# Eight state loads moved behind the first batch's softmax, and a new written order for the whole program

## The chip, the core and the metric

One core of one Trainium2 chip runs the program. Its time is device time in microseconds (us) from launch to end. The profile shows five engines: TensorE for matmuls (PE, with its weight loads PEld), VectorE (DVE), ScalarE (ACT), GpSimd (POOL) and SyncE (SP). In this kernel SP issues nearly all transfers, ACT issues two of them, and POOL issues those of the states and the stores that add to what lies in memory.

## The reference, cut to what matters

The first half is a cross attention between a sequence and a small set of states, for 8 batches and 8 heads. The second half is a gated layer on its result.

```
scores  = x @ state^T / 8           # B=8, H=8, S=512, Ns=32, D=64
a       = softmax(scores)
xread   = a @ state                 # what the sequence reads from the states
a2      = softmax(state @ x^T / 8)
sread   = a2 @ x                    # what the states read from the sequence
x2      = concat(xread, sread) -> (4352, 512) per token
h       = x2 @ w_in                 # 512 -> 2048
out     = (h * erf(softplus(h))) @ w_out   # 2048 -> 512
```

The weights arrive as 64-bit numbers and are turned into 32-bit ones in the kernel.

## The kernel before, in words

All work is cut into named steps. A step is recorded by `step(name, ...)` (L240) and emitted when its name comes up in the string `ORDER` (L20 to L169), a list of some 2,400 names. `in_order` (L1098) then ties each engine to that order, so the string alone decides which instruction stands before which on each engine; the framework adds the waits that the data need. An entry such as `~2*20` emits 20 matmuls of the identity into bank 2 of PSUM: their results are not used.

The steps that matter here, with their lines in the profile:

- `lx0` to `lx3` (L332) load batch 0 of x, 256 KB each, two on ACT's queue and two on SP's; `lst0` (L337) loads the states of batch 0.
- `x0` to `x3` (L435) transpose x on PE, `x0c` to `x3c` copy the results to SBUF, `s0` and `s0c` (L442) do the same for the states, `q0` and `q1` (L450) are the scores, `tm0`, `tm1`, `ta0`, `ta1` and later `tw0`, `tw1` (L455) are further transposes.
- `max`, `less`, `exp`, `sum`, `inv`, `norm` make the softmax of batch 0, in two halves, on DVE with `exp` on ACT. `norm1` is the last of them. `ta0c` and `ta1c` copy the transposed weights into `y` on ACT.
- A piece of w_in (`i0` to `i7`) or of w_out (`o0` to `o7`) is loaded in two halves of 512 KB on SP (`l0`, `l1`, L380) into one of four raw buffers, then converted by two ACT steps (`a0` L392, `a1` L395) and two DVE steps (`v0` L397, `v1` L399). A raw buffer is loaded again only when its `v1` has read it. `i0` is converted in two parts.
- `n00`, `n01`, `n02`, `n10`, `n12` (L935) multiply the states of batch 0 with pieces of w_in; `h0` to `h7` (L946) make the first hidden block from them and from `y`; each `h` has a softplus (`h0s`, L672) and a copy (`h0c`) on ACT. The banks of `h0`, `h1`, `h2` are used again by `h3`, `h4`, `h5`, so `h3` waits for `h0s` and `h0c`.
- `hold` (L463) is a copy of one column on POOL that reads the transposed x. Behind it on POOL stand `lst1` to `lst8` (L356): the states of batches 1 to 7, one load of 56 KB for each head. `u0` and `u1` (L1031) transpose these states on PE and need all eight loads.
- `rd0` to `rd7` (L519) are the reads `a2 @ x`. For batches 1 to 7 the weights of the read go to memory and back (`kz` L590, then four loads `z`), so `rd` waits for the last `z`. The tile `sn` holds the result of `rd0`.
- `a1xq` to `a7xq` (L345) load x a second time in another layout, sixteen transfers of 64 KB for a batch, in the place where batch 0's transposed x lay; `a1s` (L544) are the scores of batch 1.
- The rest is the two blocks of hidden units, A (batches 1 to 7) and B (0 to 7): `A1m` (L634), `A1f` (L683), `A1p` (L733, L804) and so on, on PE, with their sums on DVE and their softplus, erf and copies on ACT.

The code around the moved steps before the change:

```
            if i == 0:
                step("hold", lambda: nc.gpsimd.tensor_copy(out=sn[:, 0, 0:1], in_=xT0[:, 0, 0, 0:1]))
                for h in range(H):
                    step("lst%d" % (h + 1), load_st, h)
```

Of the kernel before, what the change touches and what calls it, by code (L numbers as in the profile page):

```python
# [20 lines left out]
warm lst0 lx0 lx3 lx2 lx1 i0l0 i1l1 i0l1 s0 x0 x3 x0c s0c i1l0 hold x3c x1 lst4 lst6 x2 x1c i2l0  # L21
lst7 q0 x2c lst2 i0a0 lst5 q01c q1 i2l1 i0a1 q00c lst1 i0v0 tm0 q11c big0 lst3 q10c i0v1 tm1 i3l0
lst8 max0 n00 max1 i0+a1 i3l1 less0 i0+a0 o0l0 less1 n00c0 exp0 i0+v0 exp1 sum0 i1a0 sum1 inv0
i1a1 inv1 norm0 norm1 ~2*20 ta0 i2a0 i1v0 ta1 n00c1 i1v1 ta0c i2a1 i0+v1 ~0*3 n02 ta1c i2v0 o0l1
n02c0 big1 ~6*1 n01 o1l0 i3a0 h0 o1l1 i2v1 n01c0 i3a1 n01c1 o2l1 big i3v0 n10 wt0 o2l0 u0 i3v1
a1xq1 n10c0 wt1 u1 n10c1 h0c wz n12 wn1 n12c1 n12c0 a1xq5 o0a0 wn0 ~4*3 tw1 n02c1 u1c o0a1 tw0
o0v0 h2 y01 tw0c o0v1 tw1c o1a0 rd0 a1xq6 t01 o1a1 o1v0 a1xq0 h1 y02 rn0 a1xq7 o1v1 o2a0 rt0 a1xq4
u0c T1 a1xq3 h0s a1xq2 h1s o2v0 ~6*8 h3 h1c a1tx0 h2c a1x2 h2s o3l0 h4 o2a1 i4l1 a1tx2 i4l0 rc0
y04 h3c i5l0 a1tx3 h5 h3s t02 h4s a1tx1 h4c t04 o2v1 a1s h5s h6 t11 a2xq3 h0e h7 a1c1 h0g a1c0
a2xq5 h4e a1my1 o00 a2xq0 a1tu1 h5c h2e a1my0 yl0 a1tu0 a2xq7 o20 h7c h2g a2xq1 a1mx1 o10 h7s i5l1  # L30
a1mx0 h6s o3l1 a1sb1 a2xq4 A1m a1sb0 h4g a1ex1 a2xq6 a1ex0 h6c a1sm1 o22 i4a1 a1sm0 a1ms a1iz i4a0
a1nm0 a1x3 o12 a1ta0 A1m00 a1ey1 i4v0 a1x0 A1f01 a1nm1 A1m10 A1m11 o02 y11 a1ta1 A1m01 a1x1 A1f0c
A1M1 a2xq2 o3a0 a1ty1 A1f02 y12 a1ey0 A1M2 A1f05 i4v1 A1f0c11 A1f06 o3a1 A1f11 a1ty0 i4k A1f0u2
y14 o14 a1kz i5a1 A1M3 y13 a1iy y03 yk1 A1M4 A1f07 i6l0 o3v0 h6e o04 o3v1 A1f0u3 i5a0 A1f0c22
A1f04 h6g a1z1 A1f03 a1z3 a1z2 o24 a1z0 A1f0c12 A1f0s11 i6l1 i5v0 A1f0c21 A1f0s22 i5v1 A1f15 A1f1c
A1f0s12 A1f16 T2 A1f0s21 i5k i7l1 rd1 t3k T4 t1k o06 A1e0 rn11 rn10 a2tx0 rt1 A1f12 A1f1u2 a2x2
a2tx2 o0c A1f17 rc1 i6a0 o0d A1g0 a2s t2k yk0 A1f1u3 t0k i6a1 o30 a3xq5 i6v0 a2c1 i7l0 A1f1c22
a2c0 A1f14 i6v1 A1f13 a2tu0 A1f1s22 i6k o32 a3xq0 A1f1c11 A1f1c12 A1f1c21 yl1 A1f1s11 a2mx0 o16
a3xq2 A1f1s21 A1f1s12 T3 o5l1 o34 a2my0 A1e1 a2x3 o5l0 a2sb0 o26 a3xq4 a2ms A1g1 o36 a2ex0 i7a0
a2sm0 A2m a2x0 o3c i7v0 i7a1 a2iz A1p10 a2nm0 a2x1 A2m10 a2ey1 i7v1 A2m00 A1p11 A2m11 a2ta0 o4l0  # L40
o1c o4l1 o5a1 i7k A2M1 A2f01 a3xq7 y21 A2m01 A2M2 A2f05 A2f0c y22 o2c A2M3 A2f06 a2ey0 a2ty1 A2f02
y23 A2f0u2 a2ty0 A2f07 A2f0c11 y24 a2kz A1A1 A1pc A2f11 a3xq3 A2f0u3 o4a1 A2f0c22 a3xq1 A2f04 A2M4
A1p50 o4a0 A1A2 a3xq6 A2f0c21 o4v0 o1d A2f03 A2f1c a2z0 a2iy o4v1 a2z3 A2f16 a2z2 a2z1 A1p60
A2f0s11 a3tx0 o4k A2f1u2 yl2 A2f0s22 o6l1 A2f0c12 o2d A2f0s12 A2f17 A1A3 o6l0 A2f0s21 A2f12 A2f1u3
A1A4 rd2 o5a0 A2f15 rn21 a3x0 rn20 a3tx2 rt2 A2f1c11 A2f14 rc2 A2f1c22 a3s o5v0 A2f1s11 o5v1 A2f13
a3x3 a3c1 o3d A1p61 a3c0 A2f1c12 t4k A2f1c21 o7l1 a3my0 A2f1s22 a3x1 A2f1s21 A1p20 t6k a3tu0
A2f1s12 a3mx0 A1p21 a4xq4 A2e1 a3sb0 o5k A3m a4xq1 A1pu2 a3ms A2g1 A2e0 o7l0 a4xq0 A1p70 a4xq7
A2g0 A1p71 a3ex0 a4xq5 o6a0 A1p51 a3sm0 a4xq6 A1pu3 o6v0 A3m00 A1p40 a3iz o6a1 A1pc22 a3nm0 a3ey0
A1p41 A3m10 o6v1 a3ey1 A3m11 a3ta0 A1p30 o6k A3m01 a3x2 A1pc11 A3M1 a3iy A3f01 y31 a3ty0 A1p31
A3M2 A3f0c o7a1 y32 y33 A3M3 A3f06 o7a0 a3ty1 A3f02 A3M4 A3f0u2 a3kz y34 A3f05 A3f0c11 a4tx2 A3f07  # L50
o7v0 A3f11 A3f0u3 A2A3 A2p10 A3f0c22 A3f0s11 a3z0 A2A1 a3z2 A3f04 yl3 A1pc12 t5k A2p11 A3f0c21
a4xq3 t61 o7v1 A3f1c A1pc21 a3z1 A3f16 yk3 A3f0s12 A2A2 a3z3 A3f0s22 A3f12 A1d1 A3f1u2 A1d2 t62
A3f03 t03 a4xq2 A3f1c11 t51 t41 A3f17 A3f1s11 A1d3 A3f0c12 A2pc A2p50 t31 A3f0s21 t21 t42 A3f1u3
A2A4 A3f15 t52 A3e0 rd3 t44 A3f1c22 t22 A3f14 t32 a4x2 rn31 rn30 t34 A3f13 a4tx0 rt3 A3f1s22 A2p51
t24 A3f1c21 A3f1c12 rc3 A3f1s12 t54 t12 A2p60 A3f1s21 t64 A3g0 A2p61 A3e1 t33 t14 a4s t43 A2pu2
A3g1 A2p70 a4c1 a5xq6 a4c0 A1d0 yk2 a4tu0 A2p71 a4x3 a5xq5 A3A1 A4m A2pu3 a4mx0 t53 a4x1 A2p20
a4sb0 a5xq7 A2pc22 a4ex0 A2p40 a4my0 a5xq1 A4m10 A4m11 a4sm0 A4m00 A2p41 A4M1 a4iz A4M3 A2p21
A2pc21 a4nm0 A4m01 t23 A2p30 A2pc11 a4ta0 A2d0 a5xq4 A4M2 A4f01 y41 a5xq0 a4ms A4M4 A2p31 a4ey0
y43 a5xq3 A4f0c y42 a4ty0 a4ey1 A4f06 y44 a4ty1 A4f02 A4f0u2 A3A2 a4kz A3ap10 a4x0 A4f0c11 A2d2
a4iy A3A4 A4f07 a5xq2 A4f05 A3A3 A4f0u3 A4f11 A4f0c22 A2d3 A4f04 a5tx2 A4f0s11 a4z1 A4f03 a4z3  # L60
A4f0c21 a4z2 A2pc12 a4z0 A3ap11 A4f1c A4f0c12 A2d1 A4f16 t13 A4f0s21 A3b1 A3ac A4f12 A4f1u2 t63
a5tx0 A4f15 A4f1c11 A4f0s12 A4f17 A3a1 rd4 A4f1u3 A3b3 A4f0s22 A4f14 a5x3 rn41 rn40 A4f1c22 rt4
A3ap50 A3a2 A4e0 A4f13 A3a3 A3ap60 rc4 A3a4 A3ap61 a5s A4f1s22 A4f1c12 A3au2 A4g0 A4f1c21 A3ap20
a6xq7 A4f1s21 A3ap70 a5c1 a6xq2 a5c0 A3ap71 A3b2 A4f1s12 a6xq5 A4f1s11 A3ap21 a5tu0 A3au3 a5x2
A3ap51 o7k A3ac11 a5my0 a6xq3 A3ap40 A3ac22 A3ap41 A4e1 a5mx0 A3bp10 a5x1 A3b4 A3bp11 a6xq1 A3ac21
a5sb0 A3ap30 A3bc A3ap31 a5ms A4g1 a5x0 A3bp60 a6xq6 a5ex0 A3bp61 A5m A3bu2 a5sm0 yl4 a6xq0 A3b4+
a5iz A3bp20 A3ac12 A5m10 a5nm0 A5m11 A3d0 A3bp21 a5ey0 a6xq4 A3bp50 A5M1 A5m01 A3bp51 a5ta0 A5m00
A3bp70 a5ey1 A3bp71 A5M2 A5f01 y51 A3bu3 A3D0 a5iy A5M3 A3bp40 A5f0c A3bc22 A3bp41 a5ty1 A5f02 y52
a5ty0 A5f06 A5f0c11 y53 a5kz A4A3 A3bp30 A3d3 A5f0u2 A3bc21 A3bp31 A5M4 A3bc11 A5f07 y54 A3bc12
A5f05 A5f0u3 A4A1 A4ap10 A3U2 A5f11 a5z3 A5f0s11 A5f0c22 a5z2 A3d2 A5f04 a6tx2 a5z1 A5f03 a5z0  # L70
A5f0c21 A4A2 A4ap11 A5f1c A3U3 A5f16 A4ac a6tx0 A5f12 A3D2 A5f1u2 A5f0c12 A4ap20 A4A4 A5f0s21
A5f17 A5f0s12 A4a1 A5f15 A5f1u3 A5f0s22 rd5 A3U4 A5f1c22 A5f14 rn50 rn51 A5e0 A4a3 A4ap21 A4a2 rt5
A5f13 rc5 A4ac11 a6s A5g0 A4ap60 a6c1 a7xq1 a6c0 A4ap61 A5f1c12 A5f1c21 yk4 A3d1 A4bp10 a6tu0
A4au2 a7xq6 A5f1c11 A4bp11 A4a4 A4ap70 yk5 a7xq0 A4ap71 a6mx0 A5f1s22 A5f1s12 A4ap50 a6my0 A5f1s11
A4ap51 A4au3 A3D1 a6sb0 a6x1 A4ap40 a7xq2 A3D3 A4ap41 A4ac22 a6ex0 A4b1 A4ap30 a6x0 A4ac21 a6sm0
A4ap31 A4bc A6m A4b2 a6x2 yl5 a6ms a6iz a6ey0 A4b4 A4b3 A4bp60 A6m00 A6m10 a6nm0 A4bp61 a6ey1
A4bp20 A4ac12 A4bu2 A4bp21 a6ta0 A4bp70 A4d2 A4bc11 A4d0 A4bp71 a7xq3 A4b4+ A4bp50 a6iy a6ty1
A5f1s21 a6ty0 A6f01 A6m11 y61 A4bu3 a6kz A4bp51 A6M1 A6m01 a6x3 A4bp40 y62 A6f0c a7xq7 A6M2 A4D0
A4bp41 A6M3 A6f02 A4bc22 A5e1 A6f06 y63 A6M4 A4bp30 y64 a7tx0 a6z3 A6f0c11 A4bp31 a6z2 A6f0u2
A6f05 a6z1 A5g1 a6z0 A6f07 a7xq4 A5ap10 A6f0u3 a7xq5 A6f11 A6f0c22 yk6 A5A3 A4d3 A6f04 A6f0s11  # L80
# [96 lines left out]
def kernel(  # L177
# [8 lines left out]
    nc = tc.nc  # L186
    B, H, S, D = x.shape
# [27 lines left out]
    big = sb("big", 12800)  # L215
# [928 lines left out]
```

## Time and profile before

| | |
|---|---|
| three timed runs, median (lowest to highest) | 697.61 us (697.14 to 698.43) |
| the profiled execution's own time | 698.53 us |
| its span, first to last instruction | 696.8 us |
| what lies around the span | 1.7 us |
| PE busy | 686.2 us (98%) |
| DVE busy, ACT busy | 583.0 us (84%), 487.3 us (70%) |
| POOL busy | 67.4 us (10%) |
| granted TensorE clock, mean of the span | 0.995 |

In the page, busy time is given for each engine with its share of the span. A timeline line gives start, duration, engine, line, operation, output<-input and count, and in square brackets how long the engine was idle before it and what ended that idle time. The ends of matmuls are modelled, so the distance between starts says more than the busy time of PE. A 32-bit matmul shows as two records; a transpose shows as one.

### The profile page before, as it was taken

What the parts mean: (1) busy time and instruction counts of PE and PEld (TensorE: products, weight loads), DVE (VectorE), ACT (ScalarE), POOL (GpSimd) and SP (SyncE); (2) the same over time, 40 slices, a digit from 0 to 9 for tenths busy, and PEclk for the clock granted to TensorE, in tenths of its full rate; (3) what the DMA queues carried; (4) which work ended last, traced back from release to release, by engine and by line L of the source; (5) the groups of instructions that cost most, each with busy time, mean ns of one, the idle gap of its engine ahead of it and who ended that gap; (6) DMA issues with size and microseconds to landing.
All of it is one profiled execution on the core that took longest, in us unless ns stands there. A gap on an engine that the chain in (4) does not pass through costs nothing.

```text
span 696.8 us, 13280 instructions
## 1 busy us (share of the span) xinstructions
PE 686.2 (98%) x5357; PEld 585.7 (84%) x5357; DVE 583.0 (84%) x761; ACT 487.3 (70%) x725; POOL 67.4 (10%) x67
## 2 busy tenths in 40 slices
PE   8899999999999999999999999999999999999997
PEld 7445557787898888899998879898999898998996
DVE  5789998999999999999935779797869796959772
ACT  4799999986696877967236785868576867575720
POOL 3000000000000200220200003020201020111002
PEclk9899999999999999999999999999999999999999
DMA  9988999865657595872456245142432323222516
GB/s 271 280 217 230 283 266 279 206 188 116 167 115 178 121 232 123 163 194 52 71 189 205 62 122 61 54 50 65 47 83 22 78 34 82 33 52 29 101 46 120
DMA packets 144028, 92.09 MB, mean 132 GB/s; under 512 B 92512, under 2 KB 135008, under 8 KB 143712
## 3 DMA queue, kind: packets, MB, share of 16 engines
q1 hardware_dynamic: 129536, 77.16, 39.3%
q0 software_dynamic: 13888, 13.57, 15.5%
q8 instruction: 42, 0.69, 0.4%
q10 hardware_dynamic: 544, 0.52, 0.2%
q14 instruction: 18, 0.15, 0.1%
HBM read 51.12 MB, written 40.11 MB: 131 GB/s over the span
## 4 chain that ended last, share of the span: by engine, by line
PE 84%; ACT 6%; DMA 4%; DVE 3%; SPq 2%; issue 1%; DVEq 0%; ACTq 0%
PE b L804 38%; PE b L683 23%; PE b L733 13%; PE b L1007 4%; PE b L634 4%; DMA ring<-in_moe_w_in_dram 2%; DMA big<-in_x_dram 1%; PE b L519 1%; ACT ring L672 1%; PE b L946 1%; PE b L544 1%; SPq L380 1%; ACT big L395 1%; ACT ring L242 1%; ACT L672 1%
## 5 line engine op out<-in xcount | busy, mean ns | idle before, releaser
L242 ACT COPY ring<-b 128x512 f32<-128x512 f32 (+1 forms) x140 | 80.3, 583 | 74.3 <-PE b L683 59.6
L683 PE MATMUL b<-y,m 128*128 128x256 f32 x480 | 121.3, 380 | 0.0
L711 POOL DMA_DIRECT2D out_dram<-res x52 | 61.6, 1415 | 610.0 <-DVE y L242 203.5
L804 PEld LDWEIGHTS b<-big,ring 128*128 128x128 f32 x928 | 111.5, 192 | 5.7 <-ACT big L582 0.8
L804 PE MATMUL b<-big,ring 128*128 128x128 f32 x928 | 115.1, 275 | 0.0
L242 ACT COPY res<-b 128x512 f32<-128x512 f32 (+2 forms) x118 | 61.2, 528 | 74.7 <-PE b L804 49.1
L683 PEld LDWEIGHTS b<-y,m 128*128 128x128 f32 x480 | 86.9, 190 | 13.4 <-issue 1.3
L683 PE MATMUL b<-sy,m 128*128 128x256 f32 x360 | 91.8, 382 | 0.0
L236 DVE TENSOR_TENSOR ring<-ring 128x2048 f32<-128x2048 f32 (+1 forms) x36 | 77.7, 2164 | 15.2 <-ACT ring L691 8.0
L235 DVE TENSOR_TENSOR ring<-ring 128x1024 f32<-128x1024 f32 (+2 forms) x80 | 86.4, 1086 | 0.3
L672 ACT ACTIVATE ring<-ring 128x512 f32<-128x512 f32 x128 | 77.1, 631 | 4.8 <-DVE ring L234 4.3
L683 PEld LDWEIGHTS b<-sy,m 128*128 128x128 f32 x360 | 64.9, 190 | 10.0 <-issue 0.9
L234 DVE TENSOR_TENSOR res<-res,b 128x512 f32<-128x512 f32 (+2 forms) x56 | 33.8, 604 | 41.0 <-PE b L804 17.5
L234 DVE TENSOR_TENSOR ring<-ring,b 128x512 f32<-128x512 f32 (+1 forms) x71 | 46.8, 660 | 24.9 <-PE b L683 8.0
L733 PE MATMUL b<-ta,ring 128*128 128x256 f32 x280 | 64.3, 381 | 0.0
L804 PEld LDWEIGHTS b<-ta,ring 128*128 128x128 f32 x496 | 60.1, 192 | 3.4 <-issue 1.7
L804 PE MATMUL b<-ta,ring 128*128 128x128 f32 x496 | 62.5, 276 | 0.0
L733 PEld LDWEIGHTS b<-ta,ring 128*128 128x128 f32 x280 | 52.5, 190 | 11.2 <-ACT res L242 2.7
L804 PE MATMUL b<-big,ta 128*128 128x128 f32 x476 | 59.5, 276 | 0.0
L804 PEld LDWEIGHTS b<-big,ta 128*128 128x128 f32 x476 | 56.8, 192 | 3.0 <-issue 2.5
L691 ACT ACTIVATE ring<-ring 128x2048 f32<-128x2048 f32 x30 | 57.1, 1911 | 0.3
L242 ACT COPY b<-b 128x512 f32<-128x512 f32 (+2 forms) x61 | 33.3, 548 | 20.5 <-PE b L733 6.8
(147 smaller groups left out, 1006.1 us busy)
## 6 DMA issues: line engine op xcount, KB each, us to landing
out_dram<-res POOLq DMA_DIRECT2D x48, 256.0 KB, 5.0
out_dram<-res SPq DMA_DIRECT2D x32, 256.0 KB, 3.5
big<-in_x_dram SPq DMA_DIRECT2D x30, 256.0 KB, 4.9
big<-in_x_dram SPq DMA_DIRECT2D x112, 64.0 KB, 3.4
big<-in_moe_w_in_dram SPq DMA_DIRECT2D x12, 512.0 KB, 6.8
big<-in_moe_w_out_dram SPq DMA_DIRECT2D x12, 512.0 KB, 5.7
kept_y<-y SPq DMA_DIRECT2D x8, 512.0 KB, 3.8
y<-kept_y SPq DMA_DIRECT2D x8, 512.0 KB, 3.9
```

Of the source, the lines that this page charges most:

```text
L234: add = lambda o, a, b: tt(o, a, b, op=ALU.add)
L235: sub = lambda o, a, b: tt(o, a, b, op=ALU.subtract)
L236: mul = lambda o, a, b: tt(o, a, b, op=ALU.mult)
L242: do[name] = lambda: f(*args)
L634: pe.matmul(out=to[j][k][Ns * p:Ns * p + Ns, :], lhsT=by, rhs=w_in[r, 4 * j:4 * j + 4, i, :], start=True, stop=True)
L672: act.activation(out=o, in_=i, func=ACTF.Softplus)
L683: pe.matmul(out=to[:, i], lhsT=xs[n - 1][:, q:q + P], rhs=ys[n - 1], start=(start and i == 0), stop=(i == 1), skip_group_check=True)
L691: step(u + "e%d" % o, lambda s=s: act.activation(out=s, in_=s, func=ACTF.Erf))
L711: nc.gpsimd.dma_start(out=to, in_=of, accum_op=ALU.add)
L733: pe.matmul(out=to[:, E2 * h:E2 * h + E2], lhsT=a[:, k // 2, k % 2], rhs=rhs[n][:, k], start=(start and h == 0 and k == 0), stop=(k == 3), ...
L804: pe.matmul(out=out_[:, P * j:P * j + P], lhsT=lhs[:, i], rhs=rhs[:, i], start=(start and j == 0 and i == 0), stop=(i == 1), skip_group_ch ...
L1007: pe.matmul(out=to[:, P * i:P * i + P], lhsT=xs[n - 1][:, i, k], rhs=ys[n - 1][:, k], start=(start and i == 0 and k == 0), stop=(k == 1), ...
```

## The change

Two steps of code and the written order.

```
@@ attention0
             step("x%d" % i, turn, i)
             ...
-            if i == 0:
-                step("hold", lambda: nc.gpsimd.tensor_copy(out=sn[:, 0, 0:1], in_=xT0[:, 0, 0, 0:1]))
-                for h in range(H):
-                    step("lst%d" % (h + 1), load_st, h)
...
             step("ta%dc" % g, act.copy, y[0][:, g], tp[g])
+        step("hold", lambda: nc.gpsimd.tensor_copy(out=sn[:, 0, 0:1], in_=A0[:, 1, 0, 0, 0:1]))
+        for h in range(H):
+            step("lst%d" % (h + 1), load_st, h)
```

`hold` now reads the normalized weights of the first batch (`A0`, second half), so it and the eight state loads behind it on POOL wait for `norm1`.

The string `ORDER` is another one from the first name to the last. It holds the same steps, apart from the unused matmuls: 35 before (in five places) and 43 after (in six places). Its beginning before:

```
warm lst0 lx0 lx3 lx2 lx1 i0l0 i1l1 i0l1 s0 x0 x3 x0c s0c i1l0 hold x3c x1 lst4 lst6 x2 x1c i2l0
lst7 q0 x2c lst2 i0a0 lst5 q01c q1 i2l1 i0a1 q00c lst1 i0v0 tm0 q11c big0 lst3 q10c i0v1 tm1 i3l0
lst8 max0 n00 max1 i0+a1 i3l1 less0 i0+a0 o0l0 less1 n00c0 exp0 i0+v0 exp1 sum0 i1a0 sum1 inv0
i1a1 inv1 norm0 norm1 ~2*20 ta0 i2a0 i1v0 ta1 n00c1 i1v1 ta0c i2a1 i0+v1 ~0*3 n02 ta1c i2v0 o0l1
n02c0 big1 ~6*1 n01 o1l0 i3a0 h0 o1l1 i2v1 n01c0 i3a1 n01c1 o2l1 big i3v0 n10 wt0 o2l0 u0 i3v1
a1xq1 n10c0 wt1 u1 n10c1 h0c wz n12 wn1 n12c1 n12c0 a1xq5 o0a0 wn0 ~4*3 tw1 n02c1 u1c o0a1 tw0
o0v0 h2 y01 tw0c o0v1 tw1c o1a0 rd0 a1xq6 t01 o1a1 o1v0 a1xq0 h1 y02 rn0 a1xq7 o1v1 o2a0 rt0 a1xq4
u0c T1 a1xq3 h0s a1xq2 h1s o2v0 ~6*8 h3
```

and after:

```
warm lx0 lx1 lx3 lx2 lst0 i0l0 i0l1 x0 i2l0 x1 x0c x3 x1c s0 i2l1 x3c x2 s0c q0 x2c i1l0 i0a0 q00c
~7*2 q1 q01c i0a1 i0v0 tm0 i1l1 q10c big0 q11c i0+a0 i0v1 tm1 i0+a1 max0 i3l0 n00 max1 less0 i3l1
less1 exp0 o0l0 i0+v0 exp1 sum0 n00c0 i2a0 sum1 inv0 inv1 i2a1 norm0 norm1 ~2*21 ta0 i1a0 i0+v1
hold ta1 big1 lst7 o0l1 i1a1 i1v0 lst3 n00c1 lst8 ta1c i1v1 ta0c lst6 i3a0 lst4 ~0*8 n01 i2v0 o1l1
n02 lst1 big o1l0 n01c0 i2v1 n02c0 lst5 i3a1 ~2*3 h0 lst2 i3v0 o2l0 o0a1 n01c1 o2l1 n02c1 a1xq7
i3v1 n10 wt0 h1 n10c0 n10c1 wt1 y01 h0c a1xq2 wz n12 wn0 n12c0 n12c1 o0a0 wn1 ~2*3 tw0 y02 tw1
o1a0 u0 tw0c tw1c u1 o1a1 a1xq6 rd0 u1c a1xq0 o0v0 h2 o2a0 u0c a1xq3 rn0 o0v1 a1xq1 rt0 o1v0 a1xq5
h0s o2v0 h1s ~6*6 h3
```

In the loads, x's four transfers now come first and the states of batch 0 last of them; the first four pieces of w_in come in the order i0, i2, i1, i3 (before: i0 and i1 mixed, then i2, i3). On ACT the conversion of i2 now stands before that of i1, and `ta1c`, `ta0c` behind both. On PE, `h1` moves ahead of `n12`, and `u0` and `u1` move from behind `n10` to behind `tw1`.

For the later reads the distance in the order also changes. PE's own time (its steps' durations in the trace of before, waits for `z` left out) between the name `kz` and the name `rd` is 7.8, 8.7, 13.0, 9.7, 11.9, 10.2 and 8.5 us for batches 1 to 7 before, and 8.7, 8.8, 9.6, 8.7, 10.2, 10.8 and 10.2 us after.

## Prediction

> **What bounds the kernel now.** The page comes first, then the list of waits of PE.
>
> ```profile
> span 696.8 us, 13280 instructions
> PE 686.2 (98%) x5357; PEld 585.7 (84%) x5357; DVE 583.0 (84%) x761; ACT 487.3 (70%) x725; POOL 67.4 (10%) x67
> ```
>
> ```profile
> PE b L519 <- DMA big<-kept_z: 1.8, 2, 1.1
> PE b L417 <- ACT y L242: 1.1, 1, 1.1
> PE b L935 <- DVE w_in L399: 1.0, 2, 0.6
> PE b L417 <- PEq L1128: 0.8, 1, 0.8
> ```
>
> PE is the bound, and its named waits are few and early; those of L519 (`rd1`, `rd2`) are at 75 and 113 us. From there to 690 us I find in the trace, by the distance between the starts of matmuls, no wait at all: 128x256 stand 216 ns apart, 128x128 112 ns, and only changes of matmul shape cost more, which the change does not remove. So nothing after 115 us can be gained, and I read the start by windows.
>
> ```profile
> 15.00:20.00 5.00, 4.34 (x46) 3.32 (x45) 4.82 (x11) 2.29 (x3) 0.00 (x0) 1.00 1.10 303
> 20.00:25.00 5.00, 3.22 (x23) 1.49 (x21) 3.58 (x6) 5.00 (x9) 0.00 (x0) 0.69 1.04 398
> 25.00:30.00 5.00, 5.00 (x43) 2.02 (x42) 2.39 (x5) 2.43 (x8) 0.00 (x0) 0.63 1.02 310
> 30.00:35.00 5.00, 4.94 (x83) 3.29 (x83) 4.61 (x10) 5.00 (x7) 0.00 (x0) 1.00 0.58 94
> ```
>
> The columns are the stretch, its length, busy time of PE, PEld, DVE, ACT and POOL, the granted clock, the DMA share and GB/s. Two things are to be seen: transfers are full (1.0 and more) until 30 us, and the clock is 0.69 and then 0.63. At half rate that is 0.31 x 5 / 0.5 = 3.1 us and 0.37 x 5 / 0.5 = 3.7 us, one stretch from about 21.9 to 28.7 us. The timeline shows what stands there:
>
> ```profile
> 19.45 1.15 ACT L392 ACTIVATE w_in<-ring 128x1024 f32<-128x1024 f32 x1 [2.71 <-DMA ring<-in_moe_w_in_dram]
> ...
> 21.12 0.49 PE L417 MATMUL b<-ident 128*128 128x128 f32 x2 [1.11 <-ACT y L242]
> ...
> 23.22 3.78 PE L946 MATMUL b<-y,m 128*128 128x512 f32 x4
> ...
> 28.07 0.37 ACT L242 COPY m<-b 128x256 f32<-128x256 f32 x1 [2.29 <-PE b L935]
> ...
> 31.68 1.98 PE L946 MATMUL b<-y,m 128*128 128x512 f32 x4
> ...
> 36.61 1.28 ACT L672 ACT_TABLE_LOAD   x1
> ...
> 37.90 1.09 ACT L672 ACTIVATE ring<-b 128x512 f32<-128x512 f32 x2
> ...
> 38.56 1.98 PE L946 MATMUL b<-y,m 128*128 128x512 f32 x4
> ```
>
> ACT waits 2.71 us for the second half of i2. Behind it stands `ta0c`, so `h0` starts at 23.22. It then runs at half rate (3.78 against 1.98 us for the same matmuls at 31.68), and ACT waits 2.29 us for `n10` behind it. From 28.07 ACT works without a pause until `h0s` (37.90), which releases `h3` at 38.56. PE covers that wait with 8 unused matmuls (2.0 us).
>
> **The change, part by part.** In both orders the same steps stand ahead of `h3` on PE and ahead of `h0s` on ACT. So the gain is the time by which these two come earlier. I walk through the new order with durations from this trace.
>
> *Loads.* The eight state loads shared the queue while i1 and i2 came: halves of 512 KB land 1.5 us apart when alone, but from 11.4 to 19.4 us only three landed. Without them the halves land at 8.4 (as now), 9.9, 11.4, 12.9 (i2 whole), 14.4, 15.9 (i1), 17.4 and 18.9 (i3).
>
> *Softmax.* DVE has the same steps and stands still only 1.1 us in all before `norm1` ends at 17.34. x now lands ahead of the states of batch 0, so `x1` waits less but `s0` more. I put both ends at -0.5 and +0.4 us and take 17.25.
>
> *ACT.* `exp1` ends as now near 14.6, then n00c0, i2 and i1 (four steps of 1.15) end at 18.9, `ta1c` and `ta0c` (0.57 each) at 19.8, against 22.58 now. No wait for a load is left.
>
> *PE.* `n01` needs these copies: 19.8. `n02` needs i1's v1 (DVE, 20.5), 3 unused matmuls, `h0` at 21.75 at full clock until 23.5 (now 26.9), `n10` 24.1, `h1` 25.8, `n12` 26.4, 3 unused matmuls 27.1, `tw0`, `tw1` 28.0.
>
> *State loads.* `hold` waits for `norm1`. On POOL nothing but the eight loads is behind it, on SP nothing moves past them. Now they run from 6.8 to a last landing of 18.5 (last issue 11.2 plus 7.3): 11.7 us. From 17.4 that is 29.1. So PE stands still about 1.1 us ahead of `u0`, `u1`, and these end at 30.0. But `rd0` needs `tw1c`: ACT does i3, wt, h0c, n12c (with waits of 0.3 and 0.85), o0a0 and o1a0 first, and ends `tw1c` at 30.3. The landing costs 0.3 us at most.
>
> *Up to `h3`.* `rd0` 30.35 to 31.4, `h2` to 33.3, `rt0`, 6 unused matmuls 1.5 us: 34.9. On ACT `o1a1`, `o2a0` end at 32.5, the table load adds 1.3, `h0s` ends at 34.4. So `h3` starts at 34.9, 3.7 us earlier, `h0s` 4.1 us earlier. Against ACT's idle times: 2.7 + 2.3 + 0.3 = 5.3 us go, 1.15 come, 4.15 remain.
>
> *From there.* Work up to `A2m` and `A3m` is the same set of steps on PE, ACT and DVE in both orders, and ACT has the same number of table loads. ACT is 97% to 99% busy from 40 to 100 us, so it can't win more; it can follow, as its own start is 4.1 us earlier. The reads after `kz`: the last `z` lands 10.8, 10.8, 11.2, 10.0, 9.0, 9.8 and 6.9 us after `kz` in this trace. The new distances, with the 0.4 to 1.0 us by which `kz` runs ahead of its name, are 9.3 to 11.5. That leaves waits of perhaps 1.8 us in all, as now; I take no change, bounds -1.8 and +2.
>
> **Sum:** 698.5 (profiled execution) - 3.7 = 694.8. The median of the timed runs is 0.9 below the profiled one; from it, 693.9. I forecast **694.0**; bounds of the forecast alone, from -0.5/+0.4, +/-1.9 and 0 to +0.3: 691.6 to 696.2.
>
> [...] The half rate came after a stretch in which PE stood still about 2.4 of 3.4 us (18.5 to 21.9). [...]
>
> **Rivals.**
> 1. *The half rate moves* to 28.7 or later (chance 0.12). For it: PE stands still about 1.4 us between 28 and 30.4. Against it: 2.4 of 3.4 us were needed now. Price: 6.8 us at half rate cost 3.4 where PE bounds: 694.0 + 3.4 = 697.4, or 696 where ACT bounds.
> 2. *The state loads starve* (0.17). They now share the queue with o0 to o2 and then the sixteen small loads of batch 1, where before they met i1 and i2. Each us beyond 29.4 goes onto `h3`: its start is the landing plus 5.7. At 32 us 696.5 (0.10). From a landing of 33 us on nothing is gained, and **slower** begins at 34.5; behind all loads of batch 1, near 36, it gives 694.0 + 6.6 = 700.6 (0.07). For it: now, too, the first state packet moved 4.4 us after its issue, when the queue was full.
> 3. *DMA can't follow* (0.12): transfers are 0.77 to 1.13 full from 40 to 113 us and now have to come 3.7 us earlier; their pauses at 30 to 40 us give 3.7 us and must all be used. If not, reads and conversions wait and the gain is given back: 697.6.
> 4. *The loads were not the reason* (0.03): i2 stays late, ACT's idle time stays: 697.5.
>
> Forecast 0.56. **Chances:** below 696.2 (0.2%, about what a measurement of this kernel can tell from no change): forecast 0.54, rival 1 0.06, rival 2 0.10, rival 3 0.06: 0.76. Within 0.2%: 0.12. Slower: rival 2 0.07, rival 3 0.04, rival 1 0.01: 0.12. Range 691.4 to 697.8: it takes in rivals 1, 3 and 4 and leaves out starved loads and a larger gain.
>
> **What would show it.** Right: ACT's wait on L392 of 2.7 us gone, full clock from 20 to 30 us, `h0` (L946) near 21.8, `h3` near 34.9, `rd1` near 71.5. Wrong: a clock under 1 in a window before 45 us (rival 1); PE waiting at L1031 for more than 1.5 us (rival 2); L519 waiting for over 3.8 us in all or ACT waiting for raw buffers between 40 and 113 us (rival 3).

## The result and the profile after

The changed kernel takes 703.34 us (median of four runs, 701.63 to 703.76), the kernel before 697.52 us in the same comparison (697.14 to 698.43). The ratio is 1.0077, with a 95% interval from 1.0057 to 1.0096: 5.4 us slower by the ratio (the medians lie 5.8 us apart), where 3.6 us faster was forecast. Code behind the moved `hold` has a line number lower by one (L519 is now L518, L946 is L945, L733 is L732); in the experiments the numbers are 3 to 5 lower than in the kernel before.

The page of the changed kernel, first lines:

```profile
span 701.7 us, 13330 instructions
PE 686.3 (98%) x5373; PEld 586.5 (84%) x5373; DVE 581.0 (83%) x761; ACT 486.3 (69%) x725; POOL 68.2 (10%) x67
```

The span is 4.9 us longer and PE is as busy as before: the time is lost in waiting and behind the last matmul. The windows of the start (columns as in the prediction):

```profile
20.00:25.00 5.00, 5.00 (x60) 2.37 (x61) 5.00 (x10) 3.86 (x6) 2.84 (x4) 1.00 1.01 285
25.00:30.00 5.00, 3.79 (x33) 1.95 (x31) 1.92 (x7) 4.49 (x10) 0.00 (x0) 1.00 1.08 296
```

The clock is full where it was 0.69 and 0.63, and the stretch of half rate is gone. The timeline of PE there, at the steps that the prediction named:

```profile
21.66 1.88 PE L945 MATMUL b<-y,m 128*128 128x512 f32 x4
...
30.07 0.95 PE L1030 MATMUL b<-ident,st 128*128 128x128 f32 x7 [1.21 <-DMA st<-in_state_dram]
30.95 1.10 PE L518 MATMUL b<-big,ring 128*32 128x64 f32 x64
...
35.69 4.56 PE L945 MATMUL b<-y,m 128*128 128x512 f32 x10 [0.27 <-ACT ring L671]
```

`h0` starts at 21.66 (before 23.22), `u0` waits 1.21 us for its states, `rd0` starts at 30.95 (before 33.59) and `h3` at 35.69 (before 38.56). The start did what it should, 2.9 us of it. On ACT the wait of 2.71 us for i2 is gone, but three waits for pieces of w_out are new; `h3` is released by ACT:

```profile
23.65 1.18 ACT L395 ACTIVATE big<-big 128x1024 uint32<-128x1024 uint32 x1 [1.14 <-DMA big<-in_moe_w_out_dram]
...
28.80 1.12 ACT L392 ACTIVATE ta<-big 128x1024 f32<-128x1024 f32 x1 [0.51 <-DMA big<-in_moe_w_out_dram]
...
32.56 1.17 ACT L392 ACTIVATE ta<-ring 128x1024 f32<-128x1024 f32 x1 [0.56 <-DMA ring<-in_moe_w_out_dram]
```

I then followed single steps through both traces, each by its start, at places where both orders have done the same work. After minus before: `h3` -2.9, `A2m` -1.8, `A3m` (at 124 us) -2.2, `B0m` (at 380 us) +0.6, `B7m` (at 629 us) +0.6, last matmul +1.5, end of the span +4.9. So 2.8 us are lost between `A3m` and `B0m`, where the kernel before has no wait of PE, 0.9 us between `B7m` and the last matmul (a wait of 0.59 us at 664.3 us for a copy on ACT is among them), and 3.4 us behind the last matmul.

**The loss in the middle.** The list of waits of PE, whole run:

```profile
PE b L518 <- DMA big<-kept_z: 2.6, 3, 1.8
PE b L1030 <- DMA st<-in_state_dram: 1.2, 1, 1.2
```

The longest, 1.8 us, is that of `rd5`. Between `A3m` and `B0m` there is one more named wait, 0.4 us for a piece of w_in at 363.7 us; the rest of the 2.8 us I can't place. The timeline of SP's and POOL's issues around `rd5` shows where its wait comes from:

```profile
200.56 2.27 SPq L345 DMA_DIRECT2D big<-in_x_dram  x2
209.43 0.91 SPq L712 DMA_DIRECT2D out_dram<-res  x2
210.39 2.25 SPq L345 DMA_DIRECT2D big<-in_x_dram  x4
212.69 0.49 SPq L607 DMA_DIRECT2D kept_y<-y  x1
213.15 1.27 POOL L710 DMA_DIRECT2D out_dram<-res  x1 [190.31 <-DVE m L235]
213.28 1.30 SPq L345 DMA_DIRECT2D big<-in_x_dram  x2
214.62 0.59 SPq L340 DMA_DIRECT2D big<-in_x_dram  x1
215.67 0.37 SPq L589 DMA_DIRECT2D kept_z<-big  x1
...
228.31 1.10 PE L518 MATMUL b<-big 128*32 128x64 f32 x64 [1.77 <-DMA big<-kept_z]
```

SP issues nothing from 202.8 to 209.4 us: the next in its order is the store `A3d2` (L712), whose data are not ready, and the loads `a6xq4`, `a6xq6`, `a6xq0` (L345) and `a5x3` (L340) stand behind it. In the order of before, this store stands behind `a5kz`. The windows of DMA there (share and GB/s are the last two columns):

```profile
205.00:210.00 5.00, 5.00 (x47) 5.00 (x46) 4.97 (x8) 3.65 (x8) 0.00 (x0) 1.00 0.01 1
210.00:215.00 5.00, 5.00 (x43) 4.90 (x43) 4.70 (x9) 2.48 (x7) 1.27 (x1) 1.00 0.93 254
215.00:220.00 5.00, 5.00 (x33) 4.64 (x33) 5.00 (x8) 2.02 (x4) 0.00 (x0) 1.00 1.14 228
```

A hole of five us, and then everything at once: `kz` of batch 5 (L589) is issued into full transfers. Before, there is no such hole, and the transfers are half empty when `kz` is issued (at 218.85 us):

```profile
205.00:210.00 5.00, 5.00 (x55) 4.33 (x61) 4.59 (x5) 4.64 (x6) 0.00 (x0) 1.00 0.76 152
...
215.00:220.00 5.00, 5.00 (x34) 4.38 (x33) 4.96 (x11) 2.16 (x5) 1.27 (x1) 1.00 0.52 78
```

The list of DMA issues from 205 to 226 us gives its time to landing, first of after and then of before:

```profile
kept_z<-big SPq DMA_DIRECT2D x1, 512.0 KB, 6.8
```

```profile
kept_z<-big SPq DMA_DIRECT2D x1, 512.0 KB, 3.3
```

**The loss at the end.** The timeline of DVE, POOL and SP from 683 us on, after:

```profile
683.74 1.02 DVE L234 TENSOR_TENSOR ring<-ring,b 128x512 f32<-128x512 f32 x2 [9.05 <-PE b L732]
...
686.41 1.82 DVE L234 TENSOR_TENSOR res<-res 128x512 f32<-128x512 f32 x2
...
688.53 3.68 POOL L710 DMA_DIRECT2D out_dram<-res  x3 [20.88 <-DVE res L234]
...
689.19 7.09 SPq L872 DMA_DIRECT2D out_dram<-ring  x8
```

DVE stands still for 9.05 us: the next in its order is `B7w5`, which needs the second half of a product of `B7` (`B7p51`) that the new order puts behind four other halves. `B6U4`, `B6C12` and `B6C2` stand behind it, and the three adding stores of `B6` (`B6d3`, `B6d1`, `B6d2`, L710) need those. So they go out at 688.53, at the same time as the eight last stores of `B7` (L872). That these three could have run earlier is a reading of the order here; an experiment below tests it. Before, POOL issued the adding stores of `B6`, four of them, ten us earlier:

```profile
678.49 4.91 POOL L711 DMA_DIRECT2D out_dram<-res  x4 [25.53 <-DVE res L234]
...
687.03 7.06 SPq L873 DMA_DIRECT2D out_dram<-ring  x8
```

The eight last stores, from issue to landing, by the list of issues from 684 to 702 us, after and then before:

```profile
out_dram<-ring SPq DMA_DIRECT2D x8, 128.0 KB, 4.3
out_dram<-res POOLq DMA_DIRECT2D x3, 256.0 KB, 7.8
```

```profile
out_dram<-ring SPq DMA_DIRECT2D x8, 128.0 KB, 1.8
```

The median rises from 1.8 to 4.3 us, the longest landing of the eight from 1.8 to 6.4 us. Transfers run until 699.3 us in after and until 695.1 us in before, and the span ends 2.4 and 1.7 us behind that. So in after the eight stores that SP issued land late beside the three that POOL issued at the same time; in before POOL has issued all of its own by 683.4 us, 3.6 us ahead of the first of the eight.

### The profile page after: what moved, and what is told of

It reads as the page before. It is cut to its first block, busy times and chain, and to the rows that moved or that the text cites. A ratio compares the mean times of both kernels' runs of the same rounds, so it can differ in the third digit from the quotient of the medians.

```text
span 701.7 us, 13330 instructions
## 1 busy us (share of the span) xinstructions
PE 686.3 (98%) x5373; PEld 586.5 (84%) x5373; DVE 581.0 (83%) x761; ACT 486.3 (69%) x725; POOL 68.2 (10%) x67
## 4 chain that ended last, share of the span: by engine, by line
PE 80%; DMA 10%; ACT 4%; DVE 2%; SPq 2%; issue 1%; DVEq 0%; ACTq 0%
PE b L803 35%; PE b L682 22%; PE b L732 13%; PE b L633 3%; PE b L1006 3%; DMA ring<-in_moe_w_out_dram 3%; DMA big<-in_moe_w_in_dram 1%; DMA w_in<-kept_in 1%; DMA big<-kept_z 1%; DMA kept_in<-res 1%; PE b L945 1%; DMA kept_z<-big 1%; DMA out_dram<-res 1%; PE b L543 1%; PE b L518 1%
## 5 line engine op out<-in xcount | busy, mean ns | idle before, releaser
L710 POOL DMA_DIRECT2D out_dram<-res x52 | 61.4, 1345 | 607.9 <-DVE m L235 190.3
L235 DVE TENSOR_TENSOR ring<-ring 128x1024 f32<-128x1024 f32 (+3 forms) x80 | 86.6, 1087 | 0.2
L682 PEld LDWEIGHTS b<-sy,m 128*128 128x128 f32 x360 | 65.4, 190 | 10.2 <-ACT b L242 1.0
L732 PE MATMUL b<-ta,ring 128*128 128x256 f32 x280 | 64.5, 381 | 0.0
L732 PEld LDWEIGHTS b<-ta,ring 128*128 128x128 f32 x280 | 52.6, 190 | 11.2 <-ACT res L242 2.5
## 6 DMA issues: line engine op xcount, KB each, us to landing
out_dram<-res POOLq DMA_DIRECT2D x48, 256.0 KB, 4.6
out_dram<-res SPq DMA_DIRECT2D x32, 256.0 KB, 3.0
big<-in_x_dram SPq DMA_DIRECT2D x30, 256.0 KB, 4.7
```

The source lines that it names most:

```text
L235: sub = lambda o, a, b: tt(o, a, b, op=ALU.subtract)
L682: pe.matmul(out=to[:, i], lhsT=xs[n - 1][:, q:q + P], rhs=ys[n - 1], start=(start and i == 0), stop=(i == 1), skip_group_check=True)
L710: nc.gpsimd.dma_start(out=to, in_=of, accum_op=ALU.add)
L732: pe.matmul(out=to[:, E2 * h:E2 * h + E2], lhsT=a[:, k // 2, k % 2], rhs=rhs[n][:, k], start=(start and h == 0 and k == 0), stop=(k == 3), ...
```

## The experiments

My theory after the two traces: the start gains 2 to 3 us, as predicted; the new order loses 2.8 us in the middle by the order of SP's queue, and 3 to 4.5 us at the end by the order of DVE's. Rivals: the start's gain was lost to transfers anyway (the prediction's rival 3); the moved state loads or the half rate decide; an adding store, not the queue, holds `kz`. Every run has its own runs of the kernel before beside it: 698.51, 698.3, 698.27 and 698.55 us (medians) in the four groups. Ratios are against those, with 95% intervals in brackets. Moved steps are shown as diffs of the written order. "From after up to X" means after's order as far as the name in front of X, and behind it all other steps in the order of before. Steps are placed by one profiled execution of each kernel.

### The order cut at `h3`

```
 ORDER: from after up to h3, then before
```

> The new order up to h3 (with the state loads behind norm1), then the order of before. Theory A (the new beginning is a real gain of 2.9 us at h3, and all that was lost was lost at later places of the new order): 697.5 - 2.9 = 694.6 us, h3 near 35.7, the last matmul near 690. Theory B (DVE, ACT and transfers can't follow an earlier start, so the gain is given back whatever order stands behind it): 697 to 698 us, with longer waits at rd1, rd2 or for raw buffers between 36 and 115 us.

Measured: 697.99 us, 0.9998 [0.9985, 1.0011]. `h3` is 3.6 us early in its profile (the fastest of its ten executions), `o00`, 10 us behind, only 1.0 us, the last matmul 1.6 us. Its list of waits of PE says what took it back:

```profile
PE b L540 <- DVE big L239: 1.5, 1, 1.5
```

This is `a1s`, the scores of batch 1, behind the transposes of x that the sixteen loads `a1xq` bring. The earlier start did not bring these loads earlier: the last lands at 39.6 us in before, 40.0 in this run and 40.7 in after. SP issues the sixteen one after another, from 23.7 to 38.0 us in this run. The transfers are full from 25 to 30 us (1.07), but only 0.60 and 0.72 busy in the two stretches to 40 us, so the pauses that the prediction's rival 3 wanted used were not used. The order of before has `a1s` right behind `h5`. So for this cut rival 3 is right in its outcome; what it said of full transfers is not what the last of these loads met.

### After without its tail

```
 ORDER: from after up to B7m, then before
```

> The new order up to B7m, then the order of before: the new tail is undone. Theory A: the tail costs 0.85 us ahead of the last matmul (a bank that waits for a copy which waits for an adding store) and 3.4 us behind it, so 703.3 - 4.1 = 699.2 us. If the end is late only because its work comes late: 703 us.

Measured: 699.26 us, 1.0009 [0.9989, 1.0029]. Without after's tail, 4.7 us of the loss of 5.4 are gone by the ratios. What remains is no gain, although in the profile `A3m` comes 3.6 us early: `B0m` is 1.2 us late. `rd5` again waits (2.1 us, for `kept_z`), and the clock is at half rate from 227.8 to 231.3 us right behind that wait.

### Only after's tail

```
 ORDER: from before up to B7m, then after
```

> The order of before up to B7m, then the new one: the tail alone. Theory A: 697.5 + 4.1 = 701.6 us, with a span that ends 7 us after the last matmul. If the tail is harmless by itself: 697.5 us.

Measured: 703.43 us, 1.0063 [1.0038, 1.0087]. The tail alone costs 4.4 us, as theory A had it (4.1). Its DVE waits 9.05 us at the same place, and its eight last stores take 4.4 us to land.

### Three steps of DVE moved in after

```
-... B7w5 B7C110 B6U4 B7p71 B7A4 B6C12 B7p30 B6C2 ...
+... B7A3 B6U4 B6C12 B6C2 B7p20 ... B7w5 B7C110 ...
```

> The new order with three names moved: B6U4, B6C12 and B6C2 stand ahead of B7p20, so on DVE ahead of B7w5, which waits for the last part of product 5. Theory A (B6's adding stores are issued at 688.5 with the last stores and hold these up because B7w5 blocks DVE): they go out near 678 us, the last stores land 1.4 us after their issue, and 3.4 us are won: 699.9 us. Rival (the late product 5 itself delays the last stores): 703 us.

Measured: 699.32 us, 1.0011 [0.9995, 1.0026]: moving three names ahead of `B7p20` takes away 4.6 us. The timeline of POOL and SP, and the issues from 675 to 702 us:

```profile
675.73 3.68 POOL L707 DMA_DIRECT2D out_dram<-res  x3 [9.74 <-DVE res L231]
687.13 6.49 SPq L869 DMA_DIRECT2D out_dram<-ring  x8
```

```profile
out_dram<-ring SPq DMA_DIRECT2D x8, 128.0 KB, 1.8
```

The adding stores are issued 13 us earlier, and the last stores land in 1.8 us again. From the last matmul to the end the run takes 4.3 us, where before takes 4.6 and after 8.0. The cause of the end is shown. DVE still stands still at `B7w5` (6.58 us); nothing that the end waits for is queued behind it any more. The loss ahead of the last matmul stays (64.7 us from `B7m` to it, 63.9 in before).

### The state loads moved, nothing else

```
-... x0c s0c i1l0 hold x3c x1 lst4 lst6 ... lst8 ... norm1 ~2*20 ta0 ...
+... x0c s0c i1l0 x3c x1 ... norm1 ~2*20 hold lst4 lst6 ... lst8 ta0 ...
```

The code of `hold` and of the loads is after's, the rest of the order is before's.

> The order of before with one part of the change: hold and the eight state loads behind norm1, nothing else. Theory T (transfers bound the first 40 us; the state loads only change places with what is behind them, and a1s can't start before the sixteen loads of batch 1 have landed near 40 us in every order): i2 is no longer late and h3 comes 1 to 3 us earlier, but a1s starts within 1.5 us of before's 43.9 and the time is within 1 us of before. Theory C (ACT's wait for i2 and the half rate behind it are what before pays for): 3 us faster than before.

Measured: 701.26 us, 1.0043 [1.0028, 1.0058]: by itself, half of the change makes the kernel 3 us slower, which neither theory had. i2 is on time now, as theory T said, and `h0` starts at 20.82 us (before 23.22). The list of waits of PE:

```profile
PE b L1026 <- DMA st<-in_state_dram: 7.0, 1, 7.0
```

The states land at 30.3 us, as late as in after (29.9), but in before's order PE comes to `u0` at 23.4 us in this run. PE waits 7.0 us there with everything behind it, the clock is at half from 27.4 to 34.3 us, and `h3` is 3.3 us late. After has `u0` behind `tw1`, and it waits 1.2 us.

### The cut at `h3` without the new unused matmuls

```
-... q00c ~7*2 q1 ... lst4 ~0*8 n01 ... i3a1 ~2*3 h0 ... wn1 ~2*3 tw0 ...
+... q00c q1 ... lst4 n01 ... i3a1 h0 ... wn1 tw0 ...
```

> e1_start without its 16 unused matmuls ~7*2, ~0*8, ~2*3, ~2*3 (~2*21 and ~6*6 stay). Theory T: if the half rate comes back at 18 to 22 us, h3 comes 1 to 2 us later than in e1_start, but a1s waits for transfers anyway, so the time stays that of e1_start (0.5 us under before on its chip) within 0.7 us. If the clock is worth what it costs at h0 (1.8 us for h0 alone): 2 us or more slower than e1_start. If no half rate comes back, the unused matmuls are not needed.

Measured: 698.15 us, 0.9997 [0.9984, 1.001], the same as with them (0.9998). The clock falls to half in this run from 21.7 to 25.1 us, and `h3` comes at 36.3 us, 1.4 us later than with them, as theory T had it. `a1s` waits for its loads anyway (1.4 us), and nothing of it is seen at the end.

### The cut at `A3m`

```
 ORDER: from after up to A3m, then before
```

> The new order up to A3m (near 120 us), then the order of before. Theory A (up to there the new order is ahead by 2.2 us, all is lost behind it): 2.2 us faster than before. If what is ahead at A3m comes from work that the new order has put off: equal to before.

Measured: 695.85 us, 0.9971 [0.9954, 0.9987]: 2.0 us faster than before, and the best version of this study. Its page begins:

```profile
span 693.5 us, 13313 instructions
```

The span is 3.3 us shorter than before's. Step by step, `A3m` comes 3.1 us early, and `B0m`, `B7m` and the last matmul 3.3 us. What the start and the first batches win is kept to the end if the order behind 121 us stays as it was. Why the cut at `h3` fails and this one holds was not tested by itself. What fits both traces: after has `a1s` behind `h7` and not behind `h5`, so that PE has work that does not need the loads of batch 1, and `a1s` doesn't wait in this run.

### The adding store `A3D0` moved

```
-... y52 A3D0 A5f0c ...
+... a5z0 A3D0 ...
```

on top of the run with the three DVE steps moved.

> e4_w5late (new order with its tail mended, 0.8 us over before on its chip) with one more name moved: the adding store A3D0 stands behind a5z0 instead of in front of a6xq0. Theory S (an adding store on POOL's queue holds up what SP has issued: a5kz took 6.8 us to land instead of 3.3): a5kz lands within 4 us, rd5 waits under 0.5 us instead of 1.9, and the time falls by 1.9 us or more, below before. Rival (the loads a6xq0 and a5x3 ahead of a5kz hold it up): rd5 waits as before and the time stays.

Measured: 700.11 us, 1.0022 [1.0006, 1.0039]. The edit did not do what it was made for. The written order ties steps to each other on one engine only, and POOL had nothing between this store and its data, so it was issued at 215.0 us, 2.5 us ahead of `kz`, as without the edit (211.2 and 213.7). `kz` again took 6.8 us to land, and `rd5` waited 1.8 us. The run tells nothing of the store. The 0.8 us to the run without the edit lie inside both intervals.

### The new order with the old state loads

```
+... x1c hold lst4 lst6 lst7 lst2 lst5 lst1 lst3 lst8 s0 ...
-... i0+v1 hold ta1 big1 lst7 ... lst3 ... lst8 ... lst2 ...
```

in the order cut at `A3m`, with before's code of `hold`.

> The order of after up to A3m and that of before behind it, as in the run that gained 2.0 us (ratio 0.9971), but with the wait and the eight state loads where before has them (behind x0, from about 7 us on). Theory A (order and moved state loads depend on each other): the state loads again share the transfers with i2 and i1; four halves are wanted by 17 us where three arrive, so the second half of i1 lands near 19 us instead of 16.7 and n01 and h0 start 2 to 3 us later than in the run with the moved loads (h0 near 24 instead of 21.7), while u0 has its state early and does not wait. The two nearly cancel at h3 or leave a loss of 1 to 2 us: about 697.5, ratio 0.998 to 1.000. Rival B (only the order counts, the state loads could have stayed): ratio 0.997 again, h3 near 36. Rival C (only the moved loads count): no gain, 698.4 or more; the run with the moved loads alone was already 3 us slower, so C is the unlikeliest.

Measured: 698.89 us, 1.0011 [0.9995, 1.0028]. The time alone would fit rival C as well as theory A, whose 1.000 it passes by a little; rival C falls with the run above in which the moved loads alone cost 3 us, and rival B's 0.997 lies outside the interval. The mechanism is theory A's. The timeline of ACT shows the old wait at a new place:

```profile
19.62 1.12 ACT L389 ACTIVATE w_in<-big 128x1024 f32<-128x1024 f32 x1 [3.53 <-DMA big<-in_moe_w_in_dram]
```

That is i1, whose halves land at 18.3 and 19.5 us in this run and at 15.2 and 16.7 in after. `h0` starts at 25.7 and `h3` at 39.9. So the two halves of the change need each other: the moved loads alone cost 3 us, the order of the start alone gives nothing, and both together give 2.0 us.

### Only after's middle

```
 ORDER: before up to A3m, after from A3m to B7m, then before
```

> The order of before up to A3m and again from B7m on, with the order of after between them (124 to 628 us). Theory A (the three parts add up: start -2.0, middle +2.6, tail +4.6 make the +5.4 of the whole change): 701.0 us, ratio 1.0037, with rd5 waiting near 2 us for its reads and B0m to B7m 2.5 to 3 us later against A3m than in before. Rival B (the middle costs only because the start hands it work earlier than its transfers follow): with the start of before the waits at rd5 go, 698.4, ratio 1.000.

Measured: 701.06 us, 1.0034 [1.0018, 1.0051], on theory A's number, though not with its single wait of 2 us at `rd5`. The middle loses the same with before's start, so it is not that the start hands it work too early. The list of waits of PE has four at L516, the reads:

```profile
PE b L516 <- DMA big<-kept_z: 4.5, 4, 1.5
```

Two are old, `rd1` and `rd2`; the new ones are at `rd5` (0.8 us) and `rd6` (1.5 us). The three parts, 0.9971 x 1.0034 x 1.0063 = 1.0068, make the whole of 1.0077 within its interval.

### `a6xq0` and `a5x3` behind the reads

```
-... a6xq0 ... a5x3 ... a5kz ... a5z2 ... a5z0
+... a5kz ... a5z2 ... a5z0 a6xq0 a5x3
```

on top of the run with the three DVE steps moved.

> The order of after with B6U4, B6C12, B6C2 ahead of B7p20 (699.32 us when it ran, ratio 1.0011), and with the transfers a6xq0 and a5x3 behind a5z0 in SP's queue instead of ahead of a5kz. Theory A (a5kz takes 6.8 us to land because a5x3 and the second a6xq0 run ahead of it on the same DMA engines): a5kz lands about 3.5 us after its issue, rd5 waits no more or under 0.5 us, and the time falls by 1.9 us to 697.4, ratio 0.998 to 0.999. Rival B (the adding store A3D0, issued 2.5 us ahead of a5kz, holds all of them): a5kz still lands after 6 us or more, rd5 waits as before, 699.3, ratio 1.001. Rival C: a5x3 itself is late for its reader then, and a wait takes the place of the one at rd5.

Measured: 699.0 us, 1.0014 [0.9996, 1.0031], no gain. `kz` now lands in 4.6 us and `rd5` starts 1.9 us earlier against `A3m`, but only its first part. Its timeline:

```profile
225.03 0.54 PE L515 MATMUL b<-big 128*32 128x64 f32 x24
226.52 0.77 PE L515 MATMUL b<-big 128*32 128x64 f32 x40 [0.95 <-DMA big<-in_x_dram]
```

The read needs x as well, and `a5x3` is the late one now: rival C. `rd6` waits 0.6 us for x as well. So it isn't which of these transfers goes last that costs; a run below issues all of them earlier.

### The unused matmuls once more

```
-... ~7*2 ... ~0*8 ... ~2*3 ... ~2*3 ... ~6*6 h3
+... h3
```

in the order cut at `A3m`; the 21 behind `norm1` stay.

> The order of after up to A3m and that of before behind it (695.85 us, ratio 0.9971, when it ran), without the unused matmuls of its pauses ahead of h3: 2, 8, 3, 3 and 6 of them go, the 21 of softmax stay. Theory A (the half rate at 22 to 29 us costs little, as transfers and ACT bound there): the clock falls to half for 3.4 or 6.8 us somewhere between 18 and 32 us, h3 starts 0 to 1 us later, and by rd1 the time is given back to within 0.7 us: 696 to 696.6, ratio 0.997 to 0.998. Rival B (half rate costs what it takes from TensorE, half of 6.8 us): 699, ratio 1.001. Rival C (the pauses are too short for half rate): full clock, 695.5 to 696.

Measured: 697.09 us, 0.9988 [0.9971, 1.0005], against 0.9971 with them. PE stands still from 17.5 to 20.2 us, and the clock is at half from about 21.3 to 24.7 us, as theory A had it; the time lies between theory A's and rival B's. `h3` starts at 35.83 us, with the matmuls at 36.03. But that is the latest of the seven executions with after's order up to `h3`, which lie between 34.6 and 36.0 us, so this pair doesn't show that the half rate costs nothing there. The 1.2 us between the medians lie within the two intervals, and the worth of the filling, from 0 to some 2 us, is not settled.

### The loads ahead of the waiting store

```
-... a5nm0 A3d2 a5ey1 ... a6xq4 ... a6xq6 ... a6xq0 ... a5x3 A3bp30 A5M3 a5kz
+... a5nm0 a6xq4 a6xq6 a6xq0 a5x3 A3d2 a5ey1 ... A3bp30 A5M3 a5kz
```

on top of the run with the three DVE steps moved.

> The order of after with B6U4, B6C12, B6C2 ahead of B7p20 (699.32 us, ratio 1.0011, when it ran), and with the loads a6xq4, a6xq6, a6xq0 and a5x3 ahead of the store A3d2 in SP's queue. In the trace of after SP stands 6.6 us at A3d2, whose data are not ready, and the transfers are 0.01 full from 205 to 210 us; then all these loads, A3D0 and a5kz are issued within 6 us, transfers are 0.93 and 1.14 full from 210 to 220 us, and a5kz takes 6.8 us to land. Theory A (that queue is what makes rd5 wait): the hole from 205 to 210 is filled, a5kz lands within 4 us, a5x3 before 214 us, rd5 waits under 0.5 us, and B0m comes about 1.9 us earlier against A3m than in the run without this edit: 697.4, ratio 0.998 to 0.999. Rival B (the adding store A3D0 alone holds a5kz): a5kz still takes 5.5 us or more, the wait at rd5 stays over 1 us, 699, ratio 1.001. Rival C (the buffers of these loads come free only at 209 us): SP waits at a6xq4 in place of A3d2, nothing moves, 699.3.

Measured: 697.6 us, 0.9985 [0.9971, 1.0]. Theory A's number again, though the interval meets that of the run without the edit (1.0011 [0.9995, 1.0026]); the traces are clearer. The timeline of SP, the windows and the issues, as for after above:

```profile
200.57 6.33 SPq L342 DMA_DIRECT2D big<-in_x_dram  x8
206.94 0.49 SPq L337 DMA_DIRECT2D big<-in_x_dram  x1
209.42 0.92 SPq L709 DMA_DIRECT2D out_dram<-res  x2
```

```profile
205.00:210.00 5.00, 5.00 (x47) 5.00 (x46) 4.97 (x8) 3.64 (x8) 0.00 (x0) 1.00 0.58 108
210.00:215.00 5.00, 5.00 (x43) 4.90 (x43) 4.69 (x9) 2.48 (x7) 1.27 (x1) 1.00 0.63 213
215.00:220.00 5.00, 5.00 (x33) 4.64 (x33) 5.00 (x8) 2.02 (x4) 0.00 (x0) 1.00 0.90 185
```

```profile
kept_z<-big SPq DMA_DIRECT2D x1, 512.0 KB, 4.4
```

The loads fill the hole, `A3d2` is still issued at 209.42, not a moment later than in after, and `kz` lands in 4.4 us although `A3D0` is issued 2.7 us ahead of it (2.5 in after). `rd5` no longer waits, and from `A3m` to `B0m` the run takes 256.0 us where it took 257.4 without the edit and before takes 255.2. So the queue of SP was the cause and the adding store alone was not (rival B falls). Mended at both places, after's order reaches 0.9985 and not the 0.9971 of the cut at `A3m`; the two intervals overlap, and whether something is still lost is open.

### The middle alone, with both reads mended

```
 as the run with only after's middle, and
-... A3d2 ... a6xq4 ... a6xq6 ... a6xq0 ... a5x3 ... a6kz ... a6z3 A4d2 ... a6x3 ... a6z2
+... a6xq4 a6xq6 a6xq0 a5x3 A3d2 ... a6x3 a6kz ... a6z3 ... a6z2 A4d2
```

> The order of before with the middle (124 to 628 us) of after, which ran in 701.06 us (ratio 1.0034) with waits of 0.95 us at rd5 and 1.7 us at rd6. Now a6xq4, a6xq6, a6xq0 and a5x3 stand ahead of A3d2, a6x3 ahead of a6kz, and A4d2 behind a6z2. Theory A (the middle loses only by the order of SP's queue around these two reads): both waits fall under 0.4 us and the time by about 2.5 us, to 698.5, ratio 1.000. Rival B (the waits stay or move to other reads): 701, ratio 1.0035. Half of it, one wait gone and the other not, would be 699.7.

Measured: 698.24 us, 0.9997 [0.9985, 1.001], where 1.0034 was measured without the edit. Both new waits are gone, and from `A3m` to `B0m` the run takes 255.4 us, 0.2 us more than before. With before's start, the middle's loss is explained by six names of the written order.

## Why the prediction was wrong

**The start: right, a little too large.** ACT's wait for i2 is gone, the clock is full, `h0` starts at 21.66 (predicted 21.75), `h3` at 35.69 (34.9, so 2.9 us of gain and not 3.7). Two terms were off: the last state load landed at 29.9 and not at 29.1, so `rd0` came at 30.95 in place of 30.35; and "No wait for a load is left" on ACT was not so, as ACT waits 1.14, 0.51 and 0.56 us for pieces of w_out, and `h3` waits for ACT. How much of the 0.8 us this is can't be told from one execution: in the seven with after's order up to `h3` it starts between 34.6 and 36.0 us, in the four with before's order between 37.2 and 39.4. `rd1`, named as a sign at 71.5 us, starts at 74.53 (before 75.45); the two orders have different matmuls ahead of it. A slip in the sum changes nothing: the bounds as named add up to 696.6 and not 696.2.

**From there: right only with the old order behind it.** The prediction let ACT, DVE and transfers follow `h3` to the end. In the version cut at `A3m` they do: 3.3 us in the profile, 2.0 us in the timed runs [0.9 to 3.2 by the interval]. Times 697.61, its ratio is 695.6 us, inside the forecast's range, but the 3.7 us of the sum lie above the interval. In after, 0.7 us of the 2.9 are gone by `A3m`, which is less than the executions differ: with after's order up to there `A3m` lies between 120.1 and 123.8 us in seven of them, with before's between 123.0 and 125.0 in four.

**The step that failed** is the sentence "So nothing after 115 us can be gained, and I read the start by windows". That nothing could be gained there was right. But from it the prediction took that nothing would change there, and apart from the reads it did not look at the new order there, although the whole string was rewritten. Where PE has no wait, another order of the same work could only lose. No rival had this in it: all four lie within the first 115 us, and the range ended at 697.8. What the runs showed in its place, in us by the traces of all kernels on record:

| stretch | before's order there | after's order there | after's, mended |
|---|---|---|---|
| `A3m` to `B0m` | 255.0 to 255.7 (8 runs) | 257.1 to 260.0 (6) | 255.4 and 256.0 (SP's queue) |
| `B7m` to last matmul | 63.9 (10) | 64.7 and 64.8 (2) | 64.6 to 65.1 (4, the three DVE steps) |
| last matmul to end | 4.6 (10) | 8.0 and 8.1 (2) | 4.3 (4, the three DVE steps) |

In time, the middle alone costs 2.4 us (1.0034) and the tail alone 4.4 us (1.0063).

**A term that was mis-sized.** For the reads, the prediction compared the new distance from `kz` to `rd` (for batch 5 it is 10.2 us of PE's time) with the time by which the last `z` lands behind `kz` in the trace of before (9.0 us). That landing was taken as a property of the transfer. In after it was 12.5 us (215.67 to 228.2), since the transfers ahead of it had changed. The shorter distance counts too: before, `rd5` starts 12.3 us behind `kz` without a wait, so with before's distance the late landing would have cost about 0.3 us (an estimate from these rows) in place of 1.8. All waits for `z` together grew only from 1.8 to 2.6 us, inside the bound of +2, as `rd1` and `rd2` wait less.

**Nobody's term: the tail.** The largest loss, 4.3 us in the profile and 4.4 us when measured alone, came for the most part from three DVE steps among the last 30 names of the order.

**The rivals.** Half rate did not move in after (rival 1): PE's pause of 1.21 us at 28.9 to 30.1 us did not bring it, the clock is 1.00 from 25 to 35 us. It did come at 227.8 us in the run without after's tail, far outside the stretch that the prediction watched. The prediction's "2.4 of 3.4 us" of standing PE in before is a misreading: it takes in 0.67 us at 21.96 us, when the half rate had begun; ahead of it stand 0.63 and 1.11 us, 1.7 in all. The states did not starve (rival 2): `u0` waited 1.2 us where 1.1 was predicted. A late landing does cost, though: with PE's old order PE waited 7.0 us for states that landed at 30.3 us, and the kernel was 3 us slower (1.0043); in after, pieces of w_out came 0.51 to 1.14 us late to ACT. The chances of rivals 1 and 2 (0.12 and 0.17) were the author's estimates. Rival 3 is what the cut at `h3` showed, in its outcome. Rival 4 falls, as the run with the old state loads has ACT's wait back.

## What to carry to other kernels

A rewritten order has to be read to its end: where the engine that bounds a stretch has no wait, the question is not what can be gained but which instruction now stands ahead of a ready one in each engine's order, above all stores that wait for data ahead of loads on SP (`A3d2` held four loads back while SP issued nothing for 6.6 us), and steps that wait for a late product ahead of those that feed the last stores (`B7w5` held DVE for 9.05 us). A landing time taken from one trace need not hold with other transfers ahead of it: `kz` of batch 5 landed in 3.3 us in before, 6.8 in after and 4.4 with the loads issued earlier. Cut a large change at a few steps where both orders have done the same work and run the pieces: here the pieces added up to the whole, and the best one beat both kernels. Run the same beginning several times before reading a difference of 1 us from two traces.

## What the hardware showed that was not expected

- With three adding stores of 256 KB that POOL issued beside SP's last eight stores of 128 KB, the median landing of the latter was 4.3 us in after, against 1.8 without them in before; the three took 7.8 us themselves.
- Half rate for 3.4 us came after pauses of PE of 2.75 and 2.55 us in the two runs without the unused matmuls (from 17.5 and 17.6 us on) and of 2.1 us at `rd5` in the run without after's tail. Pauses of 1.8 us at `rd5` (in after and in the runs with the three DVE steps moved and with the `A3D0` edit) were not followed by it, and neither was one of 2.56 us at 100.3 us in the run with the `A3D0` edit. In before, half rate for 6.8 us (21.9 to 28.7) came after pauses of 0.63 and 1.11 us that ended at 19.35 and 21.12 us. So in these runs the length of the longest pause alone does not decide.
- Transfers differed between two executions while they were full (a share of 1.00 to 1.04 in both from 95 to 105 us). The runs with the three DVE steps moved and with the `A3D0` edit have the same order up to 200 us. In the second, ACT waits 2.9 us for a piece of w_out at 101.18 us where the first has no such wait, PE then waits 2.56 us for ACT, and `rd2` comes 3.7 us later (113.29 against 109.56). `kz` of batch 2 landed 7.4 us after its issue there and 3.5 us in the other, but `rd2` did not wait for it. The two ran on different chips.
